# Two attentions mixed by a gate: the order of scores, maxima and sums on TensorE is written in blocks of four or eight steps

## The chip, the core and the metric

The kernel runs on one core of one Trainium2 chip. The metric is the device time of one execution in microseconds (us); the comparison is between two kernels run on the same chip. TensorE is called PE below, VectorE is DVE, ScalarE is ACT, GpSimd is POOL, and SyncE, which issues most DMAs, is SP.

## What is computed

```python
g = sigmoid((x * gate_w).sum(-1))            # x: 2048 x 576
a = softmax_attention(x @ wqkv) @ wo_A       # 32 heads of 18, each with its own keys and values
b = softmax_attention(x @ wq, x @ wk, x @ wv) @ wo_B   # 32 heads of 18, one key and one value for all
out = g * a + (1 - g) * b
```

There are 64 heads in all (32 of b first, then 32 of a), each with a 2048 x 2048 matrix of scores that never leaves the core. All is float32 (the queries and keys as two rounded parts that are stacked on the rows of one operand).

## The kernel before, in words

**Stages.** First the projections (L142 `project`, L183 `project_v`) and the first row maxima; then the loop over the 64 heads, which is nearly the whole time; then a short tail (`last_sums`, and the last output projection).

**Steps.** A head is 16 steps, a step is one tile of 128 keys against all 2048 queries. So there are 1024 steps, counted by T. A step has:

- four **scores** matmuls (`step_scores`, L402), one for each 512 queries. They use the low rows of the array (operands on partitions 0 to 55), write a PSUM bank of the pool `ps_s`, which has **three**, and each is followed on ACT by an exponential (L409) from that bank into a buffer `pt` in SBUF, of which there are twelve.
- four **sums** matmuls (`step_pv`, L416) that multiply the exponentials with the values. They use all rows of the array and add into one bank, `acc`, over the 16 steps of a head. They can be cut by columns into portions (`a:b`); the four of a portion run side by side on four column strips.
- what a step 22 further on needs (`LEAD`): four **maxima** matmuls (`step_max`, L367), the same products for the row maxima that are subtracted from the scores. They use the high rows of the array (partitions 64 to 117), write a bank of the pool `ps_m`, which has **four**, and each is followed by a reduction on DVE (L376). In every second step one reduction is saved: the product of columns 512 to 1023 is replaced by a **difference product** with the difference of two key blocks (`"x"`), whose relu ACT writes to SBUF (L370); the reduction of columns 0 to 511 then adds that relu while it takes the maximum (L373, a custom DVE instruction; called y below).

A scores matmul and a maxima matmul that follow each other run side by side on the two halves of the array. I call that a **pair**. The sums need the whole array, so pairs come in **groups** between portions of sums.

**At the end of a head** (`head_out`, L426) DVE copies `acc` to SBUF (L428), and SP stores the copy; the first sums of the next head overwrite `acc`, so they wait for the copy. When all maxima of a head are there, `max_rows` takes the largest on DVE (L382), transposes it (L384), POOL splits it in two parts, and two DMAs bring it as further rows of the queries; this has six steps until it is needed.

**Output projection.** In two stretches of the loop, and in the tail, `out_proj` runs units of 12 matmuls (L542) with all rows of the array into a bank of `ps_m`. ACT copies the result of the first stretch's units (L548), DVE adds that of the second's (L554). A `todo` list holds the generator, `pull` takes a unit from it.

**What sets the order.** All is issued in the order in which the Python code calls it (a manual schedule); each engine takes its own instructions in that order, and semaphores hold an instruction until its operands and its bank are there. In the kernel before, the order within two steps is a string. `sA0` is the scores of the first step's queries 0 to 511, `mB3` the maxima of the second step's last columns, `x` the difference product, `P` the whole sums of step T-2, `h` and `H` the halves of the sums of step T-1, `Q` those sums whole, and `U` a unit:

```python
PLAIN = "sA0 mA2 sA1 mA0 sA2 mA3 P sA3 mB0 sB0 mB1 sB1 mB2 h sB2 mB3 sB3 x H"
UNIT  = "sA0 mA2 sA1 mA0 sA2 mA3 P sA3 mB0 sB0 mB1 sB1 mB2 U sB2 mB3 sB3 x Q"
ALONE = "sA0 sA1 P U sA2 sA3 U sB0 sB1 h U sB2 sB3 H U"
```

UNIT is taken for two steps with a unit due: 32 of them spread over steps 522 to 865, and one in nearly every two steps from 944 to 1007. ALONE is for the last 22 steps, in which no maxima are left. The functions follow; the loop that walks the strings is shown at their end.

Of the kernel before, what the change touches and what calls it, by code (L numbers as in the profile page):

```python
# [42 lines left out]
def gated_mix_kernel(ctx: ExitStack, tc: tile.TileContext, xT, wall, wv, wo, out):  # L43
# [279 lines left out]

    def open_ph2():
        ph1.close()
        L["pt"] = ctx.enter_context(tc.tile_pool(name="ppool", bufs=12, side="left"))
        L["work"] = ctx.enter_context(tc.tile_pool(name="work", bufs=2, side="left"))
        p2 = ctx.enter_context(tc.tile_pool(name="p2", bufs=1, side="right"))
        L["pool"] = p2
        L["ks"] = [p2.tile([P, S], F32R, name=f"ksa{i}") for i in range(2)] + [ksb]  # L330
        L["kds"] = [p2.tile([P, 512], F32R, name="kda"), kdb]
        L["oacc"] = p2.tile([P, 16, D], F32, name="oacc")
        for t in L["ks"][:2]:
            for b in (SB, MB):
                dma(t[b + 54:b + 56, :], ones_r)
# [42 lines left out]
    def max_rows(u):  # L378


        m = ms[u % 2]
        nc.vector.tensor_reduce(m[:, 0:16], MX.pop(u), axis=AX.X, op=OP.max, negate=True)  # L382
        mt = lead.tile([P, 32], F32, name="mt")
        nc.vector.transpose(mt, m)  # L384
        mh = lead.tile([P, 2, 32], F32R, name="mh")
        split(mt, mh[:, 0, :], mh[:, 1, :], nc.gpsimd, nc.gpsimd)
        md = m_d[u % 4]
        dma(md, mh.rearrange("p a f -> p (a f)"))
        for b in (SB, MB) if u > NU - 3 else (SB,):
            for a in range(2):  # L390
                dma(qs[u % 3][b + 54 + a:b + 55 + a, :].rearrange("o (i b f) -> o i b f", b=4, f=32),
                    md.rearrange("(b i) (o a f) -> o a i b f", i=32, o=1, a=2)[:, a, 0:16])
# [3 lines left out]
    def step_scores(u, i, c, alone):  # L396

        b = SB
        ps = (ps_m if alone and c < 2 else ps_s).tile([P, 512], F32, name="pm" if alone and c < 2 else "ps")
        if alone and c % 2:  # L400
            b = MB
        nc.tensor.matmul(ps, kst(u)[b:b + 56, i * P:(i + 1) * P],  # L402
                         qs[u % 3][b:b + 56, c * 512:(c + 1) * 512], start=True, stop=True)
        PT["q"] = PT.get("q", []) + [(c, ps)]
        if alone and c == 0:
            return
        for c, ps in PT.pop("q"):
            pt = L["pt"].tile([P, 512], F32, name="pt")
            nc.scalar.activation(pt, ps, AF.Exp, scale=SCALE)  # L409
            PT[u, i, c] = pt  # L410

    def step_pv(u, i, a, b):


        for j in range(4):
            nc.tensor.matmul(acc[32 * j:32 * j + 19, a:b], v_of(u, i), PT[u, i, j][:, a:b],  # L416
                             start=(i == 0), stop=(i == 15), skip_group_check=True)
        if b == 512:
            for j in range(4):
                del PT[u, i, j]  # L420
# [91 lines left out]
    def out_proj(t0, rows, first=False):  # L512

        nt = len(rows)
        oacc = L["oacc"]
        O = {}

        def load(q):
            for x, y in enumerate("hl"):
                if "end" in L:  # L520
                    O[q, y] = L["end"][y][:, 256 * q:256 * q + 256].rearrange("p (t s) -> p t s", t=1)
                    continue
                t = L["pool"].tile([P, nt, 256], F32R, name=f"oi{y}", bufs=2)
                dma(t, on_d[x][P * t0:P * (t0 + nt), 256 * q:256 * q + 256]
                    .rearrange("(t p) s -> p t s", p=P))
                O[q, y] = t

        load(0)
        yield
        w = WO[t0]  # L530
        for q in range(8):
            if q < 7:
                load(q + 1)
            o = {y: O[q, y] for y in "hl"}
            for s2 in range(2):
                st_ = 2 * q + s2
                for hf in range(2):
                    fp = ps_m.tile([P, 512], F32, name="pm")
                    n = 0
                    for a, b in PRODS:  # L540
                        for t, r in enumerate(rows):
                            nc.tensor.matmul(fp[:, 0:288], o[b][:r, t, s2 * P:(s2 + 1) * P],  # L542
                                             w[a][:r, t, 288 * hf:288 * hf + 288],
                                             start=(n == 0), stop=(n == 3 * nt - 1))
                            n += 1
                    dst = oacc[:, st_, 288 * hf:288 * hf + 288]
                    if first:
                        nc.scalar.activation(dst, fp[:, 0:288], AF.Copy)  # L548
                    elif "end" in L and hf == 0 and st_ in (2, 5, 8, 11):
                        tmp = L["work"].tile([P, 288], F32, name="tmp", tag="ol", bufs=1)  # L550
                        nc.scalar.activation(tmp, fp[:, 0:288], AF.Copy)
                        nc.gpsimd.tensor_tensor(dst, tmp, dst, op=OP.add)
                    else:
                        nc.vector.tensor_tensor(dst, fp[:, 0:288], dst, op=OP.add)  # L554
                    if "end" in L and hf:
                        dma(out[st_ * P:(st_ + 1) * P, :], oacc[:, st_, :])
                    yield
# [51 lines left out]
    def when(T, f):  # L609
        at.setdefault(T, []).append(f)  # L610
# [15 lines left out]
    for t in range(8):  # L626
        when(16 * (last_head(t) + 1) + 3, lambda t=t: slow.append(normalise(t)))
    when(16 * (NU - 1) + 2, lambda: run(normalise(8, at_end=True)))
    SEG = ((0, [P] * 4, 450, 521, 857), (4, [P] * 4, 862, 942, 1008))
    for t0, rows, Ta, Tb, Tc in SEG:  # L630
        when(Ta, lambda t0=t0, rows=rows: slow.append(prep_wo(t0, rows)))
        when(Tb - 4, lambda t0=t0, rows=rows: (todo.append(out_proj(t0, rows, first=t0 == 0)), pull(1)))
    when(950, lambda: slow.append(prep_wo(8, [P])))
    when(980, load_gates)


    at_rows = list(range(522, 843, 16)) + list(range(544, 865, 32))
    assert len(at_rows) == 32

    def due(T, t0, t1, n):  # L640
        if t0 == SEG[0][3]:
            return at_rows.count(T)
        return (n * (T - t0 + 1)) // (t1 - t0) - (n * (T - t0)) // (t1 - t0) if t0 <= T < t1 else 0


    vunits = [(st_, hf) for hf in range(2) for st_ in range(16)]
# [15 lines left out]

    FIRST = "sA0 sA1 sA2 sA3 sB0 sB1 sB2 sB3 x"
    PLAIN = "sA0 mA2 sA1 mA0 sA2 mA3 P sA3 mB0 sB0 mB1 sB1 mB2 h sB2 mB3 sB3 x H"
    UNIT = "sA0 mA2 sA1 mA0 sA2 mA3 P sA3 mB0 sB0 mB1 sB1 mB2 U sB2 mB3 sB3 x Q"
    ALONE = "sA0 sA1 P U sA2 sA3 U sB0 sB1 h U sB2 sB3 H U"
    for T in range(0, NSTEP + 2, 2):
        for f in at.get(T, []) + at.get(T + 1, []):  # L670
            f()
        M = T + LEAD
        if M % 16 == 0 and M // 16 - 1 < NU:
            max_rows(M // 16 - 1)
        alone = M >= NSTEP
        units = sum(due(t, Tb, Tc, 32) for t in (T, T + 1) for _, _, _, Tb, Tc in SEG)
        for op in (FIRST if T == 0 else ALONE if alone else UNIT if units else PLAIN).split():
            k, second, c = op[0], op[1:2] == "B", op[2:]
            if k == "x":
                if M + 2 < NSTEP:  # L680
                    step_max(*divmod(M + 2, 16), "x")
            elif k == "m":
                step_max(*divmod(M + second, 16), int(c))
            elif k == "s":
                if T < NSTEP:
                    step_scores(*divmod(T + second, 16), int(c), alone)
            elif k == "U":
                pull(min(units, 1))
                units -= min(units, 1)
            elif T >= 2:  # L690
                step_pv(*divmod(T - (2 if k == "P" else 1), 16), 256 * (k == "H"), 256 if k == "h" else 512)
                if k in "HQ" and T % 16 == 0 and T < NSTEP:
                    head_out(T // 16 - 1)
        pull(units)
        if slow and M % 16:
            for _ in range(2 if T > 1000 else 1):
                if slow:
                    try:
                        next(slow[0])
                    except StopIteration:  # L700
                        slow.pop(0)
    while slow:
        run(slow.pop(0))
    last_sums()
# [35 lines left out]
```

## Time and profile before

| | us |
|---|---|
| median of 3 runs | 2768.68 (2768.68 to 2769.95) |
| the profiled execution's own time | 2769.62 |
| its span, first to last instruction | 2767.8 |
| of that, the loop over the heads | 271.7 to 2742.0 |
| PE busy | 2755.4 |
| DVE busy | 2420.0 |
| ACT busy | 2432.1 |

The granted TensorE clock is 0.998 of full over the whole execution. Busy times count overlapping instructions once; the modelled end of a matmul reaches into the next one, so the distance between the **starts** of two instructions is what the argument below uses, not the duration of one. A row of the timeline is: start in us, length in us, engine, line, operation, output<-inputs, shape, count; where several alike follow each other on an engine they are one row, and the length is from the first's start to the last's end. In brackets stands the engine's idle time before it and what ended it.

### The profile page before, as it was taken

How to read it: one execution, taken by the hardware profiler on the slowest of the kernel's cores; microseconds unless marked ns; L12 is line 12 of the kernel's file. 1: busy time of each engine (PE TensorE's matmuls, PEld its weight loads, DVE VectorE, ACT ScalarE, POOL GpSimd, SP SyncE). 2: the span in 40 equal slices, each digit the busy share in tenths (PEclk: the TensorE clock that was granted, in tenths of full speed). 3: DMA queues.
4: the chain of work that ended last, by engine and by line, in shares of the span. 5: the costliest groups of instructions: out<-in, count | busy, mean ns of one | idle time of the engine just before them, and what ended most of it. 6: DMA issues, size and time to landing. Idle time of an engine off the chain costs nothing.

```text
span 2767.8 us, 57564 instructions
## 1 busy us (share of the span) xinstructions
PE 2755.4 (100%) x22158; PEld 1226.9 (44%) x22158; DVE 2420.0 (87%) x4495; ACT 2432.1 (88%) x4776; POOL 214.9 (8%) x349
## 2 busy tenths in 40 slices
PE   9999999999999999999999999999999999999999
PEld 7888333333333333333333444444444443334554
DVE  4347999999999999999999999999999999998873
ACT  3332999999999999999999999999999999998776
POOL 2220000011001000100110001000100010011000
PEclk9999999999999999999999999999999999999999
DMA  7762011121112111211143234232332223234412
GB/s 250 251 227 74 24 32 27 32 59 53 34 30 63 42 32 35 72 39 32 40 108 99 70 76 105 61 83 71 88 85 77 70 80 84 66 77 120 110 35 87
DMA packets 122962, 214.51 MB, mean 78 GB/s; under 512 B 53500, under 2 KB 80716, under 8 KB 111002
## 3 DMA queue, kind: packets, MB, share of 16 engines
q1 hardware_dynamic: 108256, 170.79, 23.6%
q0 software_dynamic: 9824, 35.07, 3.4%
q10 hardware_dynamic: 4608, 4.98, 0.5%
q8 instruction: 174, 2.85, 0.4%
q14 instruction: 100, 0.82, 0.1%
HBM read 137.23 MB, written 64.77 MB: 73 GB/s over the span
## 4 chain that ended last, share of the span: by engine, by line
PE 99%; DVE 0%; DMA 0%; ACT 0%; POOL 0%; issue 0%; DVEq 0%; POOLq 0%; ACTq 0%
PE ps L402 42%; PE acc L416 39%; PE ps L150 7%; PE pm L367 5%; PE pm L542 4%; PE ps L186 2%; DMA xsh<-xT 0%; PE ps L367 0%; PE pm L402 0%; DVE mx L376 0%; DVE oacc L554 0%; PE pm L569 0%; PE ps L592 0%; ACT pt L409 0%; PE pm L175 0%
## 5 line engine op out<-in xcount | busy, mean ns | idle before, releaser
L409 ACT ACTIVATE pt<-ps 128x512 f32<-128x512 f32 x4052 | 2129.8, 613 | 104.0 <-PE pm L367 46.4
L376 DVE TENSOR_REDUCE mx<-pm 128x1 f32<-128x512 f32 x3064 | 1957.0, 684 | 138.8 <-PE pm L367 95.2
L402 PE MATMUL ps<-qs,ksb 56*128 56x512 f32 x2688 | 906.9, 436 | 0.3
L367 PE MATMUL pm<-ksb,qs 54*128 54x512 f32 x2332 | 813.4, 443 | 0.0
L402 PEld LDWEIGHTS ps<-qs,ksb 56*128 56x128 f32 x2688 | 436.5, 184 | 688.4 <-ACT pt L409 669.3
L416 PE MATMUL acc<-pt,vb 128*19 128x256 f32 (+1 forms) x6144 | 592.4, 457 | 0.1
L416 PE MATMUL acc<-pt,vg 128*19 128x256 f32 (+1 forms) x5656 | 579.4, 481 | 0.4 <-DVE oe L428 0.4
L402 PE MATMUL ps<-qs,ksa 56*128 56x512 f32 x1364 | 456.3, 437 | 0.0
L367 PE MATMUL pm<-ksa,qs 54*128 54x512 f32 x1232 | 433.4, 443 | 0.0
L367 PEld LDWEIGHTS pm<-ksb,qs 54*128 54x128 f32 x2332 | 375.2, 184 | 2.2
L402 PEld LDWEIGHTS ps<-qs,ksa 56*128 56x128 f32 x1364 | 218.4, 184 | 344.2 <-ACT pt L409 316.8
L373 DVE CUSTOM_DVE_ANT_0 junk<-pm,xb 128x512 bf16<-128x512 f32 x500 | 340.3, 681 | 0.2 <-ACT xb L370 0.2
L370 ACT ACTIVATE xb<-pm 128x512 f32<-128x512 f32 x500 | 305.1, 610 | 0.0
L367 PEld LDWEIGHTS pm<-ksa,qs 54*128 54x128 f32 x1232 | 200.4, 184 | 0.7
L416 PEld LDWEIGHTS acc<-pt,vb 128*19 128x19 f32 x6144 | 104.2, 97 | 209.2 <-issue 199.1
L416 PEld LDWEIGHTS acc<-pt,vg 128*19 128x19 f32 x5656 | 96.5, 97 | 208.2 <-issue 195.4
L367 PE MATMUL pm<-kdb,qs 54*128 54x512 f32 x372 | 148.5, 399 | 0.0
L116 POOL CAST mh<-mt 128x32 fp32r<-128x32 f32 x64 | 13.4, 210 | 1696.0 <-DVE mt L384 1696.0
L154 ACT ACTIVATE phl<-ps 128x512 fp32r<-128x512 f32 x56 | 33.5, 597 | 104.4 <-PE ps L150 75.6
L160 DVE TENSOR_TENSOR phl<-ps,phl 128x512 fp32r<-128x512 f32 x56 | 38.7, 692 | 94.7 <-ACT phl L154 70.9
L150 PE MATMUL ps<-xh,wh 128*128 128x512 f32 (+1 forms) x285 | 83.7, 392 | 4.9 <-ACT xh L220 4.9
L150 PE MATMUL ps<-xh,wl 128*128 128x512 f32 (+1 forms) x285 | 82.9, 389 | 0.0
(107 smaller groups left out, 1373.6 us busy)
## 6 DMA issues: line engine op xcount, KB each, us to landing
qs<-qk SPq DMA_DIRECT2D x384, 144.0 KB
qk<-phl POOLq DMA_DIRECT2D x56, 512.0 KB, 4.1
ksa<-qk SPq DMA_DIRECT2D x132, 144.0 KB
ksb<-qk SPq DMA_DIRECT2D x66, 144.0 KB
onh<-oh SPq DMA_DIRECT2D x32, 256.0 KB
onl<-ol SPq DMA_DIRECT2D x32, 256.0 KB
oih<-onh SPq DMA_DIRECT2D x16, 512.0 KB
oil<-onl SPq DMA_DIRECT2D x16, 512.0 KB
```

Of the source, the lines that this page charges most:

```text
L150: nc.tensor.matmul(fp[:, g * i:g * i + g], w[a][:kr, k, :], X[b][:kr, k, c * 512 + g * i:c * 512 + g * i + g], start=(n == 0), stop=(n == ...
L154: nc.scalar.activation(hl[:, 0, :], fp, AF.Copy)
L160: nc.vector.tensor_tensor(hl[:, 1, :], fp, hl[:, 0, :].bitcast(F32), op=OP.subtract)
L186: nc.tensor.matmul(fp[:, 0:288], X[b][:kr, k, st_ * P:(st_ + 1) * P], w[a][:kr, k, :], start=(n == 0), stop=(n == len(PROJ) - 1))
L367: nc.tensor.matmul(pm, qs[u % 3][b:b + 54, i * P:(i + 1) * P], k, start=True, stop=True)
L370: nc.scalar.activation(MX["x", u, i], pm, AF.Relu)
L373: nc.vector.tensor_tensor_reduce(junk, pm, MX.pop(("x", u, i)), 1.0, -3e38, op0=OP.add, op1=OP.max, accum_out=MX[u][:, i, c:c + 1])
L376: nc.vector.tensor_reduce(MX[u][:, i, c:c + 1], pm, axis=AX.X, op=OP.max)
L402: nc.tensor.matmul(ps, kst(u)[b:b + 56, i * P:(i + 1) * P], qs[u % 3][b:b + 56, c * 512:(c + 1) * 512], start=True, stop=True)
L409: nc.scalar.activation(pt, ps, AF.Exp, scale=SCALE)
L416: nc.tensor.matmul(acc[32 * j:32 * j + 19, a:b], v_of(u, i), PT[u, i, j][:, a:b], start=(i == 0), stop=(i == 15), skip_group_check=True)
L542: nc.tensor.matmul(fp[:, 0:288], o[b][:r, t, s2 * P:(s2 + 1) * P], w[a][:r, t, 288 * hf:288 * hf + 288], start=(n == 0), stop=(n == 3 * nt ...
```

## The change

Three things are changed; no instruction that computes something is added or removed, but some sums are cut at other columns.

1. The order is written in longer strings and without step numbers. `s` is the next scores matmul, `m` the next plain maxima matmul, `x` and `y` the next difference product and the reduction that goes with it, a digit is so many portions of 128 columns of the sums (`4` is a whole step, and a portion may reach over the end of a step), `U` a unit. `PLAIN` is four steps and `SPARSE` eight steps with one unit (steps 522 to 777, 32 of them); `DENSE` is two steps with one unit (from 946); `ALONE` has the same order as before. In a pair now either half may come first (`ms` or `sm`).
2. The difference products stand elsewhere in the order (early in the four steps and in DENSE's first pair, where they stood last in every two steps), and with them the reductions that use them. `head_out` is called when a portion ends a head; `max_rows` ahead of the block.
3. The pool of exponentials has 14 buffers where it had 12.

```diff
-        L["pt"] = ctx.enter_context(tc.tile_pool(name="ppool", bufs=12, side="left"))
+        L["pt"] = ctx.enter_context(tc.tile_pool(name="ppool", bufs=14, side="left"))
...
-    SEG = ((0, [P] * 4, 450, 521, 857), (4, [P] * 4, 862, 942, 1008))
+    SEG = ((0, [P] * 4, 450, 518), (4, [P] * 4, 862, 942))
...
-    FIRST = "sA0 sA1 sA2 sA3 sB0 sB1 sB2 sB3 x"
-    PLAIN = "sA0 mA2 sA1 mA0 sA2 mA3 P sA3 mB0 sB0 mB1 sB1 mB2 h sB2 mB3 sB3 x H"
-    UNIT = "sA0 mA2 sA1 mA0 sA2 mA3 P sA3 mB0 sB0 mB1 sB1 mB2 U sB2 mB3 sB3 x Q"
-    ALONE = "sA0 sA1 P U sA2 sA3 U sB0 sB1 h U sB2 sB3 H U"
+    PLAIN = "ms sx 4 sm sy ms 2 ms sx 2 sm ms ms 4 sm sm sm 2 ms sm 2 ys"
+    SPARSE = "ms ms sx 4 sm ms sm 2 ys sx 2 ms sm sm 4 ys sm sx 4 ms sm sm 4 ys ms ms 3 ms ms sx 3 sm ms ms " \
+             "U ms ms sm 3 ms sy sm 3"
+    DENSE = "sx sm sm 4 sy sm sm U sm sm 4"
+    ALONE = "ss 4 U ss U ss 2 U ss 2 U"
...
+            else:
+                n = int(op)
+                while n:
+                    T, a = divmod(pos["P"], 4)
+                    k = min(n, 4 - a)
+                    step_pv(*divmod(T, 16), 128 * a, 128 * (a + k))
+                    pos["P"] += k
+                    n -= k
+                    if pos["P"] % 64 == 0 and pos["P"] < 4 * NSTEP:
+                        head_out(pos["P"] // 64 - 1)
+
+    emit("ssss ssss")
+    while pos["s"] < 4 * NSTEP:
+        T = pos["s"] // 4
+        if (T + LEAD) % 16 == 0 and (T + LEAD) // 16 - 1 < NU:
+            max_rows((T + LEAD) // 16 - 1)
+        if T >= NSTEP - LEAD:
+            emit(ALONE, 1 if T < 1012 else 0)
+        elif T >= SEG[1][3] + 4:
+            emit(DENSE, 1)
+        elif SEG[0][3] + 4 <= T < SEG[0][3] + 4 + 8 * 32:
+            emit(SPARSE, 1)
+        else:
+            emit(PLAIN)
+    emit("4 2 2")
```

The first block starts at T = 2. So a head's last sums stand at the end of a block of four or eight (or of two in DENSE), ahead of its trailing `ys` where it has one, and `max_rows` stands ahead of the block with T = 10, 26, 42 and so on.

More of the change, by code (lines that the diff above doesn't have):

```diff
@@ L628, in gated_mix_kernel @@
     when(16 * (NU - 1) + 2, lambda: run(normalise(8, at_end=True)))
-    SEG = ((0, [P] * 4, 450, 521, 857), (4, [P] * 4, 862, 942, 1008))
-    for t0, rows, Ta, Tb, Tc in SEG:
+    SEG = ((0, [P] * 4, 450, 518), (4, [P] * 4, 862, 942))
+    for t0, rows, Ta, Tb in SEG:
         when(Ta, lambda t0=t0, rows=rows: slow.append(prep_wo(t0, rows)))
-        when(Tb - 4, lambda t0=t0, rows=rows: (todo.append(out_proj(t0, rows, first=t0 == 0)), pull(1)))
+        when(Tb, lambda t0=t0, rows=rows: (todo.append(out_proj(t0, rows, first=t0 == 0)), pull(1)))
     when(950, lambda: slow.append(prep_wo(8, [P])))
     when(980, load_gates)
[L637 to L643, printed above, removed]
     vunits = [(st_, hf) for hf in range(2) for st_ in range(16)]
@@ L660, in gated_mix_kernel, with begin @@
     open_ph2()
-    FIRST = "sA0 sA1 sA2 sA3 sB0 sB1 sB2 sB3 x"
-    PLAIN = "sA0 mA2 sA1 mA0 sA2 mA3 P sA3 mB0 sB0 mB1 sB1 mB2 h sB2 mB3 sB3 x H"
-    UNIT = "sA0 mA2 sA1 mA0 sA2 mA3 P sA3 mB0 sB0 mB1 sB1 mB2 U sB2 mB3 sB3 x Q"
-    ALONE = "sA0 sA1 P U sA2 sA3 U sB0 sB1 h U sB2 sB3 H U"
-    for T in range(0, NSTEP + 2, 2):
+    PLAIN = "ms sx 4 sm sy ms 2 ms sx 2 sm ms ms 4 sm sm sm 2 ms sm 2 ys"
[3 more added lines that the diff above has]
+    ALONE = "ss 4 U ss U ss 2 U ss 2 U"
+    pos = {"s": 0, "P": 0, "x": (LEAD + 2) // 2, "y": (LEAD + 2) // 2}
+    plain = [(M, c) for p in range((LEAD + 2) // 2, NSTEP // 2)
+             for M, c in [(2 * p, 2), (2 * p, 3)] + [(2 * p + 1, c) for c in range(4)]]
+    def begin(T):
         for f in at.get(T, []) + at.get(T + 1, []):
             f()
[L672 to L695, printed above, removed]
+        if slow and T % 16 != 10:
             for _ in range(2 if T > 1000 else 1):
@@ L701, in gated_mix_kernel, with emit @@
                         slow.pop(0)
+    def emit(ops, units=0):
+        for op in ops.replace(" ", ""):
+            if op == "s":
+                if pos["s"] % 8 == 0:
+                    begin(pos["s"] // 4)
+                step_scores(*divmod(pos["s"] // 4, 16), pos["s"] % 4, pos["s"] // 4 >= NSTEP - LEAD)
+                pos["s"] += 1
+            elif op in "xy":
+                step_max(*divmod(2 * pos[op], 16), "x" if op == "x" else 0)
+                pos[op] += 1
+            elif op == "m":
+                M, c = plain.pop(0)
+                step_max(*divmod(M, 16), c)
+            elif op == "U":
+                if units:
+                    pull(1)
+                    units -= 1
+            else:
[22 more added lines that the diff above has]
+    emit("4 2 2")
     while slow:
```

## The prediction

> **What bounds the kernel now.** First the page's chain and its engines' shares, then busy time by stretch (the loop's four stages: steps 0 to 521, 522 to 865, 866 to 945, 946 to 1001), then the timeline of PE.
>
> ```profile
> PE 2755.4 (100%) x22158; PEld 1226.9 (44%) x22158; DVE 2420.0 (87%) x4495; ACT 2432.1 (88%) x4776; POOL 214.9 (8%) x349
> PE 99%; DVE 0%; DMA 0%; ACT 0%; POOL 0%; issue 0%; DVEq 0%; POOLq 0%; ACTq 0%
> ```
> ```profile
> 271.70:1483.70 1212.00, 1211.26 (x10413) 460.04 (x10410) 1163.58 (x2186) 1186.86 (x2348) 75.14 (x124) 1.00 0.18 46
> 1483.70:2333.60 849.90, 849.87 (x7012) 348.98 (x7008) 773.37 (x1445) 800.79 (x1582) 51.00 (x85) 1.00 0.31 79
> 2521.20:2695.10 173.90, 173.90 (x1236) 88.57 (x1233) 141.33 (x264) 132.32 (x252) 5.33 (x10) 1.00 0.32 79
> ```
>
> PE ends the chain, but DVE and ACT are busy 96% and 98% of the first stage (1163.58 and 1186.86 of 1212.00), so a new order can make either late for a while though neither gets more work. The stage has 261 blocks of two steps: 4.644 us each. One of them, on PE:
>
> ```profile
> 1205.19 1.05 PE L416 MATMUL acc<-pt,vb 128*19 128x512 f32 x8
> 1206.17 0.50 PE L402 MATMUL ps<-qs,ksb 56*128 56x512 f32 x1
> 1206.18 0.50 PE L367 MATMUL pm<-ksb,qs 54*128 54x512 f32 x1
> 1206.51 0.39 PE L402 MATMUL ps<-qs,ksb 56*128 56x512 f32 x1
> 1206.52 0.39 PE L367 MATMUL pm<-ksb,qs 54*128 54x512 f32 x1
> 1206.75 0.39 PE L402 MATMUL ps<-qs,ksb 56*128 56x512 f32 x1
> 1206.75 0.39 PE L367 MATMUL pm<-ksb,qs 54*128 54x512 f32 x1
> 1207.07 0.63 PE L416 MATMUL acc<-pt,vb 128*19 128x256 f32 x8
> 1207.63 0.50 PE L402 MATMUL ps<-qs,ksb 56*128 56x512 f32 x1
> ...
> 1207.97 0.39 PE L402 MATMUL ps<-qs,ksb 56*128 56x512 f32 x1
> ...
> 1208.30 0.63 PE L416 MATMUL acc<-pt,vb 128*19 128x256 f32 x8
> 1208.86 0.50 PE L402 MATMUL ps<-qs,ksb 56*128 56x512 f32 x1
> ...
> 1209.43 0.39 PE L402 MATMUL ps<-qs,ksb 56*128 56x512 f32 x1
> ...
> 1209.81 1.05 PE L416 MATMUL acc<-pt,vb 128*19 128x512 f32 x8
> ```
>
> From start to start: a portion of 512 columns takes 0.98 (1205.19 to 1206.17), one of 256 takes 0.56, so 0.42 per 256 and 0.14 fixed, and one of 384 would take 0.77. In a group the first pair takes 0.34 (1206.17 to 1206.51), a middle one 0.24, the last one 0.32. So a group of three is 0.90, of two 0.66, and the block's floor is 2 x 0.90 + 0.66 + 0.98 + 2 x 0.56 = 4.56. The other 0.08 is waiting for banks: the pair at 1209.43 takes 0.38. One turn from pairs to sums and back costs 0.14 (two portions of 256 against one of 512) and 0.34 + 0.32 - 2 x 0.24 = 0.18 (two groups against one): **0.32 us**.
>
> **Pitches of the other two engines**, and how a bank comes free:
>
> ```profile
> 1203.86 0.68 DVE L376 TENSOR_REDUCE mx<-pm 128x1 f32<-128x512 f32 x1
> 1204.45 0.68 DVE L428 COPY oe<-acc 128x512 f32<-128x512 f32 x1
> 1205.05 0.68 DVE L376 TENSOR_REDUCE mx<-pm 128x1 f32<-128x512 f32 x1
> 1205.65 0.68 DVE L373 CUSTOM_DVE_ANT_0 junk<-pm,xb 128x512 bf16<-128x512 f32 x1
> ```
> ```profile
> 1206.71 0.60 ACT L409 ACTIVATE pt<-ps 128x512 f32<-128x512 f32 x1
> ```
> ```profile
> 1206.71 1.58 ACT L409 ACTIVATE pt<-ps 128x512 f32<-128x512 f32 x3
> ```
> ```profile
> 1208.06 1.28 DVE L376 TENSOR_REDUCE mx<-pm 128x1 f32<-128x512 f32 x2
> ```
> ```profile
> 1209.39 0.18 PEld L367 LDWEIGHTS pm<-ksb,qs 54*128 54x128 f32 x1
> ```
> ```profile
> 1209.42 0.69 DVE L376 TENSOR_REDUCE mx<-pm 128x1 f32<-128x512 f32 x1
> ```
>
> DVE starts a 128x512 operation every 0.60 us and each is done 0.68 after its start; ACT every 0.49 ((1.58 - 0.60) / 2), done 0.60 after its start. A group's first scores are taken up by ACT 0.54 after their start (1206.17 to 1206.71), its first maxima by DVE 0.56 after (1208.86 to 1209.42). A bank is reloaded 0.05 after its reader's end (1208.06 + 1.28 = 1209.34, load at 1209.39), and a load that comes late costs 0.10 more (a first pair's 0.34 against 0.24).
>
> **The change part by part.** PLAIN keeps its turns: its groups are 3, 3, 2, 3, 3, 2 pairs, its portions 4, 2, 2, 4, 2, 2, twice the old block, floor 9.12 for four steps. What the new order costs or saves lies in four places.
>
> *The copy at a head's end (+33.1).* The old block recorded seven DVE operations after its last x (m y m, m m m, m) and then the copy; a pair with an x, which gives DVE nothing, was the last. PLAIN's second x is the seventh of 16 pairs; after it come `2 | sm ms ms | 4 | sm sm sm | 2 | ms sm | 2` and the copy, so eight reductions. Counted from the start of the half portion right after that x: the next group starts at 0.56, its first reduction at 0.56 + 0.56 = 1.12, and DVE is free for the copy at 1.12 + 8 x 0.60 = 5.92. The copy ends at 6.60, and the next head's sums can load at 6.65. They are due at 0.56 + 0.90 + 0.98 + 0.90 + 0.56 + 0.66 + 0.56 + 0.90 = 6.02: **PE waits 0.63**. For the old order the same count gives 1.12 + 7 x 0.60 + 0.73 = 6.05 against 6.02, so almost nothing, and the trace has 0.06:
>
> ```profile
> 1204.80 0.39 PE L402 MATMUL ps<-qs,ksb 56*128 56x512 f32 x1
> ```
>
> (0.39 to the sums at 1205.19 instead of 0.32 to 0.33.) In SPARSE DVE runs dry during the unit; from the next group's start six operations follow (`ms ms sm 3 ms sy sm 3`), the copy ends at 0.56 + 3.60 + 0.68 + 0.05 = 4.89 and the sums are due at 3 x 0.90 + 2 x 0.77 + 0.03 = 4.27: 0.62. Of the 63 copies 58 stand at the end of a block of four or eight with such a queue ahead; in DENSE and ALONE DVE has room (141.33 of 173.90). 58 x (0.63 - 0.06) = +33.1.
>
> *The largest maxima (+9.9).*
>
> ```profile
> 1186.04 0.22 DVE L382 TENSOR_REDUCE m<-mx 128x16 f32<-128x64 f32 x1
> 1186.37 0.21 DVE L384 STREAM_TRANSPOSE mt<-m 128x32 f32<-128x32 f32 x1
> 1186.50 0.65 DVE L376 TENSOR_REDUCE mx<-pm 128x1 f32<-128x512 f32 x1
> ```
>
> These two take DVE 0.46. `max_rows` now stands behind the same queue: eight reductions to 5.92, y to 6.53, these two to 6.99, then the first m of the block, done at 7.67, its bank usable at 7.82. The pair that takes this bank again (four maxima on) is due at 6.02 + 0.98 + 0.34 + 0.24 = 7.58: a wait of 0.24; without the two it would be free at 7.36. While PE is late by it, the block's other bank waits (0.07 a block) fall away, so I take 0.17: 58 x 0.17 = 9.9, between 0 and 13.9. What hangs on `max_rows` behind DVE (POOL's split, two DMAs on SP) has six steps, some 14 us, and stays ahead of its use.
>
> *x in DENSE's first pair (+8.4).* ACT takes the relu second: from the group's start, exponentials at 0.54, 1.52 and 2.01, the relu at 1.03. The third's bank is usable at 2.01 + 0.60 + 0.15 = 2.76; the third pair of the second group, which writes it, is due at 0.90 + 0.98 + 0.34 + 0.24 = 2.46: 0.30 of waiting. Before, the relu came last and those blocks had no waits: 173.90 / 28 = 6.21 against a floor of 2 x 0.90 + 0.66 + 2 x 0.98 and a unit of 1.78, 6.20.
>
> ```profile
> 2555.01 0.80 PE L542 MATMUL pm<-woh,oih 128*128 128x288 f32 x4
> ...
> 2556.79 0.49 PE L402 MATMUL ps<-qs,ksa 56*128 56x512 f32 x1
> ```
>
> 28 blocks x 0.30 = +8.4. The thirty-second unit moves from a block of two into ALONE and costs the same there.
>
> *Fewer turns in SPARSE (-8.3).* Eight steps before are three plain blocks and one with a unit: 3 x 4.56 + 6.20 = 19.88 at floor, 12 turns. SPARSE has 11: ten groups of three and one of two, portions 4 x 0.98 + 2 x 0.56 + 4 x 0.77, a unit: 9.00 + 0.66 + 3.92 + 1.12 + 3.08 + 1.78 = 19.56. 32 x 0.32 = -10.2. Two of its portions per block reach over a step's end and become two runs of four matmuls. No row shows such a break; it costs between nothing and the fixed 0.14, and I take 0.03, near nothing, as weights can load while the run before streams: 64 x 0.03 = +1.9.
>
> *Bank waits else* (0.08 a block of two) I leave as they are: the same rings, the same pitches; if they went or doubled in half of the blocks, -19 or +19. The two more buffers cost nothing: SPARSE holds up to 13 exponentials, and a portion always stands at least three exponentials behind the newest scores, as many as `ps_s` lets ACT be late.
>
> Sum: 33.1 + 9.9 + 8.4 - 8.3 = +43.1. On the profiled execution's 2769.6 (0.9 over the median of three runs): **2812.7 us**.
>
> *The order within a pair* is the unknown of this sum. Within groups the half that comes first changes five times in PLAIN and eleven in SPARSE: 172 x 5 + 32 x 11 = 1212 places where two matmuls of one half follow each other; before there were none. By the nearest rows such a place may expose 0.10 more of a load, or save as much: ±121. I take 0:
>
> ```profile
> 1206.28 0.19 PEld L402 LDWEIGHTS ps<-qs,ksb 56*128 56x128 f32 x1
> 1206.29 0.19 PEld L367 LDWEIGHTS pm<-ksb,qs 54*128 54x128 f32 x1
> ```
>
> both halves' next weights load together, 0.23 ahead of their pair and while the earlier matmul of the same half runs (1206.17, 0.50 long). The Trainium skill, page "TensorE: Matmul & The Clock Gate", section "Part 3: Packing small matmuls — row/col tiling", says that a weight load overlaps a running matmul only where its row group differs. Taken alone that speaks against the change, and gives the first rival; the rows above, where the load overlaps a matmul of its own rows, do not bear it out.
>
> **The rivals.**
> 1. *Neighbours of one half lose their overlap.* At 0.10 a place 2812.7 + 121 = 2934, at half that 2873. Against it: the loads above. Chance 0.05.
> 2. *A group gains from the changed order* (the other side). Place: the same 1212; if a load starts earlier there, each saves up to 0.10, down to 2692; half of it is 2752. It decides from 43.1 / 1212 = 0.036 us a place. For it only that a first pair has 0.10 of load left to hide; against it that middle pairs follow at 0.24 with none exposed. Chance 0.07.
> 3. *DVE keeps up, and the change does nothing.* If a reduction's pitch were under (6.02 - 1.12 - 0.73) / 8 = 0.52, the waits for the copy and the maxima would vanish, the old 0.06 with them: 2769.6 + 8.4 - 8.3 - 3.5 = 2766. Against it: every pitch above is 0.60. Chance 0.05.
>
> **How the numbers follow.** The forecast, DVE's queue at a head's end, has 0.83. Its own bounds: the maxima -10 to +4, the breaks -2 to +7, bank waits -19 to +19, which do not all fall on one side; 2794 to 2832 leaves out the rivals and little else. A measurement tells about 0.2% (5.5 us) from no change. Slower by more: 0.83 + 0.05 = 0.88; within: 0.05; faster: 0.07.
>
> **What would show it.** After: the copy (now L427) starting 0.6 to 0.8 after the head's last sums have ended, behind three reductions, and PE's weight loads for `acc` waiting about 0.6 for it, 58 times; first sums of a head 0.6 late on PE; two four-step blocks in a head at about 9.27, the one with `max_rows` at 9.4, the one with the copy at 9.8; DENSE at 6.5 a block with ACT as releaser. SPARSE blocks without a copy at 19.6 to 19.9. The forecast is wrong if DVE starts the copy at once, or if middle pairs whose order changes come at another pitch than 0.24.

## The result

The changed kernel takes **2834.46 us** (median of 4 runs, 2830.82 to 2835.95) against 2768.68 (2767.63 to 2769.95): a ratio of 1.0235, 95% interval 1.0222 to 1.0248. It is slower by 65.8 us where 43.1 were forecast, 2.5 us above the upper end of the range.

The page after: PE is busy a little longer than before (2780.3 us against 2755.4), but its share of the chain that ended last fell from 99% to 89%: DVE, ACT and transfers have shares in it.

```profile
span 2834.2 us, 58086 instructions
PE 2780.3 (98%) x22422; PEld 1244.6 (44%) x22422; DVE 2418.0 (85%) x4495; ACT 2450.9 (86%) x4776; POOL 215.3 (8%) x349
PE 89%; DVE 5%; DMA 3%; ACT 1%; issue 1%; SPq 0%; POOL 0%; DVEq 0%; POOLq 0%; ACTq 0%
```

Busy time by stretch, first the four of the kernel after, then the second and third of the kernel before (its first and fourth stand above), cut at the same steps (0, 522, 778, 946, 1002). The first column behind the stretch is its length, the next ones are PE, PEld, DVE, ACT and POOL busy; the first of the last three is the granted clock.

```profile
271.50:1516.10 1244.60, 1223.01 (x10412) 460.90 (x10410) 1162.12 (x2184) 1200.20 (x2347) 75.26 (x124) 1.00 0.17 45
1516.10:2173.50 657.40, 644.35 (x5506) 284.97 (x5502) 575.27 (x1075) 603.38 (x1186) 33.41 (x58) 0.99 0.31 77
2173.50:2577.00 403.50, 395.82 (x3364) 149.35 (x3362) 374.95 (x707) 386.50 (x756) 39.39 (x55) 1.00 0.31 80
2577.00:2759.70 182.70, 182.45 (x1234) 90.40 (x1230) 142.71 (x265) 130.33 (x254) 5.32 (x10) 1.00 0.27 78
```
```profile
1483.70:2116.60 632.90, 632.88 (x5222) 260.11 (x5218) 575.49 (x1075) 595.98 (x1177) 33.34 (x58) 1.00 0.31 78
2116.60:2521.20 404.60, 404.58 (x3402) 161.06 (x3398) 377.61 (x708) 386.94 (x766) 39.30 (x55) 1.00 0.33 83
```

The first stretch, plain blocks alone, is 32.6 us longer (1244.6 against 1212.0); DVE's busy time hardly moves, ACT's is 13.3 longer, and PE is idle there (1223.01 of 1244.60 busy; before, 1211.26 of 1212.00). The stretch of SPARSE is 24.5 longer, but it holds 32 units where the same 256 steps held 24: eight units of about 1.6 us (6.21 for a block of two steps with one, 4.64 without) are some 13 of it. The third stretch is 1.1 shorter without these eight units, so in itself some 12 longer. DENSE is 8.8 longer.

**Where PE waits.** I took from each trace the time from every group of pairs, portion and unit to the next one and subtracted its floor (the prediction's: 0.34, 0.24 and 0.32 for pairs, 0.14 + 0.42 per 256 columns, 1.78 for a unit). What is left is called waiting; it is put to a place by where it stands:

| waiting of PE in the loop, us | before | after | difference | forecast |
|---|---|---|---|---|
| first sums of a head (the copy) | 3.2 | 36.9 | +33.7 | +33.1 |
| behind the largest maxima | 0.5 | 17.2 | +16.7 | +9.9 |
| second group of DENSE | 0.0 | 8.4 | +8.4 | +8.4 |
| behind three reciprocals | 0.0 | 8.1 | +8.1 | not seen |
| all else (bank waits, breaks in a portion, order, clock) | 34.8 | 45.1 | +10.3 | +1.9 |
| sum of waiting | 38.5 | 115.7 | +77.2 | |
| loop, first to last scores | 2470.3 | 2536.6 | +66.3 | |
| so the floor (fewer turns) | | | -10.9 | -10.2 |

**The copy.** The views are PE's and DVE's timeline of the kernel after at the end of a head, then who waited for the copy.

```profile
999.84 0.63 PE L415 MATMUL acc<-pt,vb 128*19 128x256 f32 x8
1000.40 0.49 PE L367 MATMUL pm<-ksb,qs 54*128 54x512 f32 x1
...
1000.74 0.39 PE L402 MATMUL ps<-qs,ksb 56*128 56x512 f32 x1
...
1000.97 0.42 PE L402 MATMUL ps<-qs,ksb 56*128 56x512 f32 x1
1001.95 0.62 PE L415 MATMUL acc<-pt,vb 128*19 128x512 f32 x4 [0.55 <-DVE oe L427]
```
```profile
998.21 3.08 DVE L376 TENSOR_REDUCE mx<-pm 128x1 f32<-128x512 f32 x5
1001.21 0.68 DVE L427 COPY oe<-acc 128x512 f32<-128x512 f32 x1
1001.81 0.68 DVE L373 CUSTOM_DVE_ANT_0 junk<-pm,xb 128x512 bf16<-128x512 f32 x1
```
```profile
PEld acc L415 <- DVE oe L427: 51.8, 63, 0.9
PE acc L415 <- DVE oe L427: 31.9, 59, 0.6
```

The head's last sums (999.84, a half portion) give way to the next pair at 1000.40. Five reductions without a pause hold DVE until 1001.21; only then the copy starts, 0.8 after the sums, and the next head's sums follow its end (1001.89) at 1001.95, 0.98 after their last pair instead of 0.32. 59 of 63 heads have it: 0.64 in plain blocks, 0.58 in SPARSE, against a worked-out 0.63 and 0.62.

**The largest maxima.** DVE of the kernel after at a block with T = 10 of its head, then PE there:

```profile
982.33 0.68 DVE L373 CUSTOM_DVE_ANT_0 junk<-pm,xb 128x512 bf16<-128x512 f32 x1
982.93 0.09 DVE L373 DVE_READ_ACCUMULATOR2_ANT mx<- 128x1 f32 x1
983.05 0.22 DVE L382 TENSOR_REDUCE m<-mx 128x16 f32<-128x64 f32 x1
983.38 0.21 DVE L384 STREAM_TRANSPOSE mt<-m 128x32 f32<-128x32 f32 x1
983.51 1.25 DVE L376 TENSOR_REDUCE mx<-pm 128x1 f32<-128x512 f32 x2
```
```profile
983.75 0.97 PE L367 MATMUL pm<-ksb,qs 54*128 54x512 f32 x2
984.22 0.50 PE L402 MATMUL ps<-qs,ksb 56*128 56x512 f32 x1
984.65 0.63 PE L415 MATMUL acc<-pt,vb 128*19 128x256 f32 x8
```

The custom operation's place ends at 982.33 + 0.60 = 982.93, the next reduction starts at 983.51: the two small ones take **0.58**, not 0.46. About 0.1 stands ahead of each of them (982.93 to 983.05; 983.05 + 0.22 to 983.38), and each reads what the operation before it wrote; that this is the reason fits the rows, but no run tests it. The third pair comes 0.47 after the second (984.22 to 983.75) instead of 0.24, and the portion 0.43 after that instead of 0.32: 0.34 here and 0.33 in the median of the 32 such blocks of the first stretch.

**The reciprocals.** `normalise` has DVE take the reciprocal of the stored sums (L459) once in seven heads. DVE of the kernel after, who waited for its load after and before, and PE after:

```profile
1954.13 1.29 DVE L376 TENSOR_REDUCE mx<-pm 128x1 f32<-128x512 f32 x2 [0.66 <-PE ps L402]
1958.71 0.95 DVE L459 RECIPROCAL sm<-sm 112x128 f32<-112x128 f32 x1 [3.29 <-DMA sm<-sum_d]
1959.58 0.63 DVE L376 TENSOR_REDUCE mx<-pm 128x1 f32<-128x512 f32 x1
```
```profile
DVE sm L459 <- DMA sm<-sum_d: 14.1, 4, 6.8
```
```profile
DVE sm L460 <- DMA sm<-sum_d: 6.9, 1, 6.9
```
```profile
1956.37 0.84 PE L415 MATMUL acc<-pt,vg 128*19 128x384 f32 x8
1960.27 0.79 PE L367 MATMUL pm<-ksa,qs 54*128 54x512 f32 x1 [3.05 <-DVE mx L376]
...
1963.61 0.79 PE L367 MATMUL pm<-ksa,qs 54*128 54x512 f32 x1
...
1964.20 0.62 PE L367 MATMUL pm<-ksa,qs 54*128 54x512 f32 x1
...
1964.63 0.62 PE L367 MATMUL pm<-ksa,qs 54*128 54x512 f32 x1
```

One wait of 6.8 us is in the tail of both kernels; the other three are new (1.8, 3.3 and 2.3). A reciprocal whose load has not landed stands in DVE's queue ahead of reductions whose banks PE needs: PE was idle for 3.05 us behind the one shown. The cause is a line of the diff that neither the list of changes nor the forecast has: the background generators are advanced in `begin`, at a block's **start**, where they were advanced at its end. In a head without a wait there are 13.9 us from the copy to the reciprocal before (833.55 to 847.45) and 11.1 after (848.53 to 859.59 in the same head). In the three heads the reciprocal starts 11.9, 13.4 and 13.4 us behind its copy, when its load has landed: later than 11.1, and within the 13.9 that were left before. In the one shown the chain goes by a load of the output projection, ahead of the sums' way to DRAM (`sum_d`) and back:

```profile
1944.03 10.45 DMA oil<-onl
...
1955.19 1.70 DMA sum_d<-oe
1956.96 1.73 DMA sm<-sum_d
```

**The clock behind them.** Two of the three waits cost a second time. Behind the one shown the granted TensorE clock is 0.50 for 6.8 us, and behind the last one (from 2246.14) for 3.4 us; in the kernel before, the loop behind its first 10 us has no such stretch.

```profile
1959.42:1966.24 6.82, 5.97 (x32) 3.48 (x33) 5.56 (x11) 3.75 (x7) 0.46 (x1) 0.50 0.03 8
2246.14:2249.55 3.41, 3.41 (x23) 1.08 (x22) 2.87 (x7) 2.18 (x4) 0.00 (x0) 0.50 0.09 22
```

The pair at 1963.61 takes 0.59 there instead of 0.34, the one at 1964.20 takes 0.43 instead of 0.24. Behind the reciprocals' own waits, the groups, portions and the unit in these two stretches take 3.3 us more than their floors, and the table has them under "all else": PE is at work there, only slower. So the late reciprocals cost 8.1 + 3.3 = 11.4 us.

### The profile page after: what moved, and what is told of

It is laid out like the page before. It is cut to its first block, busy times and chain, and to the rows that moved or that the text cites. A ratio compares the mean times of both kernels' runs of the same rounds, so it can differ in the third digit from the quotient of the medians.

```text
span 2834.2 us, 58086 instructions
## 1 busy us (share of the span) xinstructions
PE 2780.3 (98%) x22422; PEld 1244.6 (44%) x22422; DVE 2418.0 (85%) x4495; ACT 2450.9 (86%) x4776; POOL 215.3 (8%) x349
## 4 chain that ended last, share of the span: by engine, by line
PE 89%; DVE 5%; DMA 3%; ACT 1%; issue 1%; SPq 0%; POOL 0%; DVEq 0%; POOLq 0%; ACTq 0%
PE acc L415 35%; PE pm L367 21%; PE ps L402 21%; PE ps L150 6%; PE pm L541 4%; PE ps L186 2%; DVE mx L376 2%; DMA qs<-qk 2%; DVE oe L427 1%; DVE junk L373 1%; ACT pt L409 1%; DMA ksa<-qk 0%; SPq L49 0%; DMA oil<-onl 0%; DMA ksb<-qk 0%
## 5 line engine op out<-in xcount | busy, mean ns | idle before, releaser
L409 ACT ACTIVATE pt<-ps 128x512 f32<-128x512 f32 x4052 | 2152.7, 620 | 156.7 <-PE pm L367 70.8
L402 PE MATMUL ps<-qs,ksb 56*128 56x512 f32 x2688 | 931.3, 443 | 0.3
L415 PE MATMUL acc<-pt,vg 128*19 128x256 f32 (+3 forms) x5920 | 575.0, 468 | 14.6 <-DVE oe L427 14.6
L367 PEld LDWEIGHTS pm<-ksb,qs 54*128 54x128 f32 x2332 | 368.8, 184 | 267.0 <-DVE mx L376 170.0
L402 PE MATMUL ps<-qs,ksa 56*128 56x512 f32 x1364 | 464.6, 442 | 0.5 <-ACT pt L409 0.5
L370 ACT ACTIVATE xb<-pm 128x512 f32<-128x512 f32 x500 | 313.1, 626 | 1.4 <-PE pm L367 1.4
L415 PEld LDWEIGHTS acc<-pt,vg 128*19 128x19 f32 x5920 | 107.1, 97 | 223.0 <-issue 190.7
L367 PE MATMUL pm<-kdb,qs 54*128 54x512 f32 x372 | 160.4, 431 | 1.8 <-DVE mx L376 1.8
L116 POOL CAST mh<-mt 128x32 fp32r<-128x32 f32 x64 | 13.5, 211 | 1795.7 <-DVE mt L384 1795.7
```

The source lines that it names most:

```text
L367: nc.tensor.matmul(pm, qs[u % 3][b:b + 54, i * P:(i + 1) * P], k, start=True, stop=True)
L370: nc.scalar.activation(MX["x", u, i], pm, AF.Relu)
L402: nc.tensor.matmul(ps, kst(u)[b:b + 56, i * P:(i + 1) * P], qs[u % 3][b:b + 56, c * 512:(c + 1) * 512], start=True, stop=True)
```

## The experiments

Times are medians; the kernel before was timed beside each and stayed at 2768.6 to 2769.2, so the differences to the changed kernel's 2834.5 are taken across. `-` lines are of the changed kernel, except in the two experiments on the kernel before (mixed pairs, fourteen buffers); "waits" are those of the table above, from each kernel's own trace. "..." marks lines left out.

### Scores first in every pair

```diff
-    PLAIN = "ms sx 4 sm sy ms 2 ms sx 2 sm ms ms 4 sm sm sm 2 ms sm 2 ys"
+    PLAIN = "sm sx 4 sm sy sm 2 sm sx 2 sm sm sm 4 sm sm sm 2 sm sm 2 sy"
-    SPARSE = "ms ms sx 4 sm ms sm 2 ys sx 2 ms sm sm 4 ys sm sx 4 ms sm sm 4 ys ms ms 3 ms ms sx 3 sm ms ms U ms ms sm 3 ms sy sm 3"
+    SPARSE = "sm sm sx 4 sm sm sm 2 sy sx 2 sm sm sm 4 sy sm sx 4 sm sm sm 4 sy sm sm 3 sm sm sx 3 sm sm sm U sm sm sm 3 sm sy sm 3"
```

> The changed kernel, but in every pair of PLAIN and SPARSE the scores stand first; groups, portions and places of x and y stay. Queue theory (PE waits because DVE and ACT come to the copy, the largest maxima and the bank late): nothing changes, within 3 us of the changed kernel's 2834. Rival (the 1212 places where two matmuls of one half follow each other cost TensorE time): up to 22 us faster, as that is what my sum missed; 50 or more if most of the loss were there.

2825.66 us (ratio to before 1.0206, 1.0191 to 1.0221): 8.8 faster. Of the table's rows "all else" moves, from 45.1 to 34.6, and no other by 2. (That this is just the 34.8 of before is chance: the two stretches at half clock are in this trace too.) So the order in a pair is not free, though the queue theory took it to be; it is worth about a sixth of the loss: 10 us in 1212 places, 0.008 us each on average.

### PLAIN in the old order

```diff
-    PLAIN = "ms sx 4 sm sy ms 2 ms sx 2 sm ms ms 4 sm sm sm 2 ms sm 2 ys"
+    PLAIN = "sm sy sm 4 sm sm sm 2 sm sx 2 sm sy sm 4 sm sm sm 2 sm sx 2"
...
-    emit("ssss ssss")
+    emit("ssss ssss x")
```

> The changed kernel with PLAIN in the old order (x last in every two steps, so one DVE operation fewer ahead of the copy and a dry DVE ahead of the largest maxima); one x more ahead of the loop. SPARSE, DENSE and the rest as changed. Queue theory: the plain stretches fall back to 4.64 us for two steps, 42 copies no longer wait, 2834 - 42 = about 2792. Rival (the loss is spread over units, DENSE and transfers): less than 15 us faster.

2803.67 us (1.0126, 1.0109 to 1.0142): 30.8 faster, between the two expectations. The plain stretches do what was expected, 1244.6 to 1213.9 and 403.5 to 397.0:

```profile
271.70:1485.60 1213.90, 1212.68 (x10413) 460.97 (x10410) 1163.71 (x2186) 1186.23 (x2348) 75.36 (x124) 1.00 0.18 46
1485.60:2148.20 662.60, 650.31 (x5508) 286.71 (x5504) 573.48 (x1073) 605.01 (x1186) 33.41 (x58) 0.99 0.31 77
2148.20:2545.20 397.00, 393.70 (x3366) 149.21 (x3362) 376.66 (x709) 382.13 (x756) 39.37 (x55) 1.00 0.32 81
```

SPARSE, which I had left alone, loses 5.2 (657.4 to 662.6) with an x more ahead of it, and the reciprocals' waits grow to 11.9. Of the copies those in SPARSE still wait (12.4 us for all copies). This string also puts the scores first in all pairs of PLAIN and has DVE dry ahead of the largest maxima, so the run does not tell the copy from these two.

### A copy that nothing waits for

```diff
-        nc.vector.tensor_copy(oe, acc)
+        nc.vector.tensor_copy(oe.rearrange("p (a b) -> p a b", b=32), ones.unsqueeze(1).to_broadcast([P, 16, 32]))
```

> The changed kernel, but the copy at a head's end copies a tile of ones in place of the sums (same place in DVE's order, same size; the sums of all heads but the last are left out of the output), so the next head's first sums wait for no copy. Queue theory: 58 waits of about 0.6 go, of which some 10 per cent come back as bank waits, since DVE stays behind: 30 to 37 us faster, about 2800. Rival (the copy is late only because PE is): under 10 us faster.

2806.93 us (1.0138, 1.0123 to 1.0153): 27.5 faster. The copies' waits fall from 36.9 to 1.3, and 9.3 of that comes back in "all else" (54.4). About 2 of this is the half clock, which this trace has for 17 us behind its reciprocals where the changed kernel's has it for 10; the rest is bank waits, as DVE's queue itself is as long as it was. The direction is the queue theory's and the size a little under its 30 to 37; the rival's 10 is out. This is the one run in which nothing but the copy's wait was taken out.

### x in DENSE's third pair

```diff
-    DENSE = "sx sm sm 4 sy sm sm U sm sm 4"
+    DENSE = "sm sm sx 4 sy sm sm U sm sm 4"
```

> The changed kernel with x in the third pair of DENSE's first group instead of the first. Queue theory (ACT takes the relu between the first and the second exponential, and the third bank comes back late): 28 blocks x 0.30 = 8.4 us faster, 2826, and DENSE at 6.21 a block. Rival (the wait belongs to the unit): no change.

2823.30 us (1.0195, 1.0180 to 1.0210): 11.2 faster. The stretch is back at 6.23 a block (174.4 / 28), and its waits at 0.1:

```profile
2570.10:2744.50 174.40, 174.16 (x1234) 88.66 (x1230) 141.95 (x265) 130.06 (x254) 5.33 (x10) 1.00 0.29 82
```

That is 8.3. The other 2.9 us lie in the reciprocals' waits, 4.2 in this profile instead of 8.1, and in the clock behind them, 0.50 for 3.4 us instead of 10.2. Both differ between kernels that leave the reciprocal where it is (waits of 4 to 12 us).

### The largest maxima in mid-block

```diff
-    PLAIN = "ms sx 4 sm sy ms 2 ms sx 2 sm ms ms 4 sm sm sm 2 ms sm 2 ys"
+    PLAIN = "ms sx 4 sm sy ms 2 ms sx 2 r sm ms ms 4 sm sm sm 2 ms sm 2 ys"
...
+            elif op == "r":
+                if rows_due:
+                    max_rows(rows_due.pop())
...
```

> The changed kernel, but in PLAIN the largest maxima (max_rows) are recorded after the second x of the block with T = 10, 26, ..., where DVE has run dry, not ahead of the block; SPARSE and DENSE as changed. Queue theory: the bank wait of 0.33 behind these two DVE operations goes in 42 heads, less what the second half of the block then loses: 9 to 14 us faster, about 2823. Rival (the wait in those blocks comes from the first use of a head's loaded rows): no change. Should the rows come too late for the next head (3.5 steps, 8 us, are left), PE waits on a DMA and it is slower.

2819.38 us (1.0181, 1.0167 to 1.0195): 15.1 faster. The waits behind these two operations go from 17.2 to 3.5 (what is left stands in SPARSE); that is 13.7, inside the expected 9 to 14, and about 1 more is in the reciprocals' waits. Recorded where DVE is dry anyway, 0.58 us of DVE cost next to nothing, and eight microseconds are enough for the rows' way.

### The reciprocal four steps later

```diff
-        yield
-        yield
+        for _ in range(4):
+            yield
         nc.vector.reciprocal(sm[:n, :], sm[:n, :])
```

> The changed kernel, with the reciprocal of the sums recorded four steps later behind the load of what it reads. Theory: the reciprocal, 11 us behind the copy where it was 14 before the change, stands in DVE's queue before its load has landed and holds the reductions (1.8, 3.3 and 2.3 us of DVE, 8 us of PE in three heads of the stretch with the projection's loads): 8 us faster, about 2826. Rival (those heads wait for late loads of queries or keys): no change.

2823.47 us (1.0195, 1.0180 to 1.0211): 11.0 faster. Only the tail's wait for that load is left, and the 8.1 us of PE are gone. "All else" falls by 4.4 to 40.7: 3.3 of it is the half clock, of which the loop of this trace has nothing behind its first 10 us. The expected 8 left the clock out; the 11.4 worked out above has it. The other executions agree: the granted clock is 0.998 or 0.999 in all four of this kernel, 0.996 or 0.997 in all four of the changed one.

```profile
DVE sm L459 <- DMA sm<-sum_d: 7.8, 1, 7.8
```

### SPARSE alone

PLAIN in the old order as above, DENSE in the old order (`"sm sy sm 4 sm sm sm U sm sx 4"`), the late reciprocal; SPARSE as changed.

> PLAIN and DENSE in the old order, the late reciprocal, SPARSE as changed (with one x more ahead of it): what SPARSE alone nets. Sum of the parts measured so far against before: fewer turns -10, 16 copies +9, the largest maxima there +5, changed order in pairs +3, the leading x in SPARSE +5 (seen in old_plain): +12, about 2780. Rival (SPARSE pays once the rest is undone): under 2765.

2779.34 us (1.0037, 1.0024 to 1.0051): the sum of the parts, 2780, holds. SPARSE saves its turns and gives back more.

### Fewer turns without the queue

```diff
-    SPARSE = "ms ms sx 4 sm ms sm 2 ys sx 2 ms sm sm 4 ys sm sx 4 ms sm sm 4 ys ms ms 3 ms ms sx 3 sm ms ms U ms ms sm 3 ms sy sm 3"
+    SPARSE = "sm r sx 4 sm sm sm 4 sm sm sm 2 sm sy 2 sm sy sx 4 sm sy sm 4 sm sm sm 3 sx sm sm U sm sm sm 3 sm sm sm 2 sm sx 4 " \
+             "sy sm sx 4 sm sy sm 3 sm sm sx 3 sm sy sx U sm sm sm 3 sm sm sy 3 sm sm sm 3 sy sm sx 4 sm sm sm 3 sm sm sm 3 sm sm sm 3 sm"
...
-            emit(SPARSE, 1)
+            emit(SPARSE, 2)
```

All else as in SPARSE alone; `r` is `max_rows`, which in this stretch stands in the string.

> As all_undone_but_sparse, but the stretch with the first 32 units has one string for 16 steps, with 21 portions and two units (23 turns, where the old order has 24 and SPARSE 22), scores first in every pair, the copy ahead of which DVE has room, and the largest maxima after the first pair. Queue theory: no copy and no largest maxima wait there, and the units now stand in 256 steps instead of 344: 7 to 11 us faster than the kernel before, about 2760. Rival (bank waits eat what turns save): no faster than before.

(The string has 20 portions and two units in 16 steps, 22 turns like SPARSE; the counts in the expectation are one too high.) **2762.04 us** over 8 runs, ratio to the kernel before 0.9973 (0.9963 to 0.9983): faster than both kernels. Its stretch of 256 steps with 32 units takes 636.9, where SPARSE took 657.4 and the same 256 steps before 632.9 with 24 units, and the following one 391.5 instead of 404.6, without the other eight:

```profile
1484.20:2121.10 636.90, 636.35 (x5764) 288.63 (x5762) 566.15 (x1074) 605.15 (x1185) 33.59 (x58) 1.00 0.31 80
2121.10:2512.60 391.50, 391.29 (x3364) 148.76 (x3361) 376.76 (x709) 381.79 (x757) 36.24 (x52) 1.00 0.32 81
```

Its copies wait 3.2 us in all, as before. So the gain that the longer blocks were to bring is there once DVE has room ahead of the copy and the largest maxima, and the scores stand first; these three were changed together.

### The kernel before with mixed pairs

```diff
-    PLAIN = "sA0 mA2 sA1 mA0 sA2 mA3 P sA3 mB0 sB0 mB1 sB1 mB2 h sB2 mB3 sB3 x H"
+    PLAIN = "sA0 mA2 mA0 sA1 sA2 mA3 P mB0 sA3 sB0 mB1 mB2 sB1 h mB3 sB2 sB3 x H"
```

(and the same in UNIT.)

> The kernel before, in which only the order within pairs alternates (five changes of the first half in every two steps, some 2500 in all, twice as many as in the changed kernel); DVE's and ACT's own orders stay. If a place where two matmuls of one half follow each other costs TensorE what s_first suggests (10 us in 1212 places, 0.008): 15 to 21 us slower, about 2788. Rival (the order in a pair only mattered through the waits around it in the changed kernel): within 4 us of the kernel before.

2780.93 us (1.0044, 1.0032 to 1.0057): 12.2 slower, between the two. It is a cost of its own, 0.005 us a place on average, less than the 0.008 that the changed kernel had shown. It does not fall inside the groups: over the first stretch (from 290 us on) the mean distance from the first pair of a group of three to the second is 0.337 before and 0.336 here, from the second to the third 0.234 and 0.233. It is the last pair that takes longer, 0.369 to the sums instead of 0.359, in groups of two 0.347 instead of 0.341. In the same stretch weight loads cover 503.73 us where they covered 460.04, as the two halves' loads no longer always fall together; in the last pair of one group they stand 0.20 apart, in the pair before it they coincide:

```profile
1207.82 0.19 PEld L367 LDWEIGHTS pm<-ksb,qs 54*128 54x128 f32 x1
1207.82 0.19 PEld L402 LDWEIGHTS ps<-qs,ksb 56*128 56x128 f32 x1
1208.06 0.18 PEld L367 LDWEIGHTS pm<-ksb,qs 54*128 54x128 f32 x1
1208.26 0.18 PEld L402 LDWEIGHTS ps<-qs,ksb 56*128 56x128 f32 x1
```

How much of this is the array's own and how much the waits for banks that then hold one half and not the other, these runs do not tell.

### Fourteen buffers

```diff
-        L["pt"] = ctx.enter_context(tc.tile_pool(name="ppool", bufs=12, side="left"))
+        L["pt"] = ctx.enter_context(tc.tile_pool(name="ppool", bufs=14, side="left"))
```

> The kernel before with 14 exponential buffers in place of 12, nothing else. All theories: no change (within 3 us); a gain would say that ACT had waited for buffers.

2768.83 us (0.9999, 0.9991 to 1.0008): nothing, as expected.

### Four costs taken out at once

Scores first, the largest maxima in mid-block, x in DENSE's third pair and the late reciprocal together, on the changed kernel.

> The changed kernel with four of the five costs taken out at once, as each was by itself: scores first in every pair, the largest maxima in mid-block, x in DENSE's third pair, the late reciprocal. The copy behind DVE's queue and the fewer turns stay. If the costs are separate: 10 + 13.5 + 8.4 + 8 = 40 us faster than the changed kernel, 2790 to 2795, with the copies' 33 us and the turns' -10 left over 2769. Rival (they overlap, one hides another): above 2803.

2798.36 us (1.0106, 1.0091 to 1.0121): 36.1 faster; 3 us above the expected 2790 to 2795, it lies between that and the rival's 2803. In its waits the four places are gone but for 4.2 behind the largest maxima in SPARSE (the expectation had allowed for 13.5 of 17), "all else" is 36.0, and the copies' are 38.6. The single runs' medians add up to 46.1, 10 more than the four together. In part that is the reciprocals' waits and the clock behind them, which moved in several of the single runs; in part waits came back: without the order's 10.5 and the clock's 3.3 "all else" would be 31.3, and the copies' waits rose by 1.7. So the costs are separate in the main, and overlap by some 6 us. What is left over 2768.7 is 29.7: copies 38.6 - 3.2, the 4.2, and -10.9 for the turns, 28.7.

## Why the prediction was wrong, point by point

- **Bound and method held in the main.** PE's order, worked out pair by pair with the pitches of one block, gave the time of each place whose queue had been counted with the right price.
- **The copy**: +33.1 forecast, +33.7 measured. Its cause is shown by the copy of ones, which changes nothing else; the old PLAIN and the string with DVE dry ahead of the copy agree, though they change other things too.
- **x in DENSE's first pair**: +8.4 forecast, +8.4 measured, and 8.3 undone by moving it two pairs.
- **Fewer turns**: -10.2 forecast, -10.9 in the floor. The breaks in portions: +1.9 forecast, at 0.03 each; in the trace a portion of 384 columns with a break takes 0.777 and one without 0.772 (medians), so 64 breaks cost 0.3.
- **Bank waits else**, "I leave as they are": this held within some 4 us. "All else" rose by 10.3, of which 10.5 is the order and 3.3 the clock, so the rest fell by 3.5.

Three steps failed, and together they are why the forecast was too low:

1. **The reciprocals: not seen**, +8.1 of waiting and +3.3 of half clock. The forecast followed what `max_rows` issues behind the queue, but not the generators whose advance moved from a block's end to its start. The late reciprocal took back 11.0.
2. **The order within a pair: "I take 0"**. It costs 10.5 in the waits and 8.8 in the time, by the run with scores first. The forecast's reason for 0 was that both halves' loads run ahead of their pair. The middle pairs do keep their pitch, as the kernel before with mixed pairs shows (0.233 against 0.234), but the last pair of a group does not, and the forecast did not look there.
3. **The largest maxima: mis-sized**, +9.9 forecast, +16.7 measured. The price of 0.46 was too low. In the rows at 1186.04 the forecast took the 0.11 between the reduction's place (1184.13 + 3 x 0.60 = 1185.93) and the small one for a dry DVE, but it is part of what the two cost (0.58):

```profile
1184.13 1.88 DVE L376 TENSOR_REDUCE mx<-pm 128x1 f32<-128x512 f32 x3
```

With 0.58 the count gives 0.24 + 0.12 = 0.36 where 0.33 was measured. And taking off 0.07 for bank waits that would fall away had no ground: they stayed. The range given for this term, 0 to 13.9, missed it.

Of the rivals, the first (neighbours of one half lose their overlap) had the right sign, at a tenth of its size. The Trainium skill (page "TensorE: Matmul & The Clock Gate", section "Part 3: Packing small matmuls — row/col tiling") has a weight load overlap a running matmul only where its row group differs. Taken alone, that is not what these traces show: in the kernel before, a load at 1206.28 overlaps a matmul of its own rows from 1206.17 to 1206.67, by the profile's modelled ends. The second rival (a gain there) is out, by two runs. The third (DVE keeps up) is out by the copies.

In sum: 43.1 + 6.8 (maxima) + 8.1 (reciprocals) + 8.4 (all else, 10.3 less the 1.9 forecast) - 0.1 (copy and turns) = 66.3, what the loop took more. The mechanism that the forecast named, DVE's queue at a head's end, was right and is half of the loss; what it missed was one wait, one term that it put at nothing, and one price. Each of the four smaller places was undone by itself, and together they gave 36.1.

## What to carry to other kernels

When an order is made longer or denser for one engine, count the queue of the others at every point where that engine must wait for one short operation: a copy, a small reduction or a reciprocal costs little by itself, but behind three late reductions it stops TensorE until that queue is done, 0.6 us each time here. Put such operations where their engine has just run dry, and an operation that waits for a transfer well behind it. A wait of some microseconds can cost twice: two of three here were followed by a halved clock. And follow every line of a rewritten loop, also the one that only moves background work from a block's end to its start.

## What the runs showed of the hardware that was not expected

- Two small DVE operations of 0.22 and 0.21 us, each reading what the one before it wrote, took 0.58 us of the engine: about 0.1 more ahead of each (983.05 behind 982.93; 983.38 behind 983.05 + 0.22).
- Two matmuls on the two halves of the array run side by side whichever is issued first, but changing which one comes first cost 0.005 (2500 places, 12.2 us) to 0.008 us (1212 places, 10 us) a place on average; in the kernel before it stood in the last pair ahead of the sums. How it comes about is open.
- A break inside a portion of sums (the matmuls of one step, then those of the next, at 128 and 256 columns) cost 0.005 us, so portions need not end with a step.
- After two of the three new waits, in which the profile has PE idle for 3.05 and 1.76 us, the granted clock was 0.50 for 6.8 and 3.4 us; after the third, 1.51 us, it stayed full. Three waits give no rule for when it falls.
